# Edge lines kept as sum and difference in a fused spectral mixer: narrower filter products and strided evictions

## The chip, the cores and the metric

The kernel runs on one core of a Trainium2 chip. The metric is the device time of one execution in microseconds (us); lower is better. The engines are named as in the profile: PE is TensorE (PEld its weight loads), DVE is VectorE, ACT is ScalarE, SP is the queue that issues nearly all transfers. L967 is line 967 of the kernel before.

## The reference, cut to what matters

Two branches are mixed by a gate that is computed per row. Branch A is a two-dimensional real FFT, a product with a complex filter, and the inverse FFT. Branch B is a layer norm and a two-layer network over the token axis.

```python
x = A_x                                       # [1, 2048, 512], bf16
g = sigmoid((x * gate_w).sum(-1, keepdims=True))
X = rfft2(x)                                  # over tokens S = 2048 and features D = 512
X = X * (w_r + 1j * w_i)                      # filter [2048, 257]
a = irfft2(X, s=(S, D))
h = layernorm(B_x)
u = gelu(einsum("bsd,sf->bdf", h, w1) + b1)   # F = 1792
b = transpose(einsum("bdf,fs->bds", u, w2) + b2)
out = g * a + (1 - g) * b
```

## The kernel before, in words

The 2048 tokens are split as q (4) x position (128 partitions) x r (4), so there are 16 row blocks of 128 rows, numbered j = 4q + r. Every step of the kernel is added as a task with an engine, a duration that the author has set, what it reads and writes, the PSUM banks it takes (`fa`, `fb`, `acc`) and a priority. A list scheduler (`Plan.order`) then writes out the order of all engines from these. So an edit of a duration can move instructions on every engine. `mm(...)` is the duration of a group of matmuls.

The network is two runs of 512-column matmuls: `m1` (L705, 16 row blocks for each of 14 tiles of hidden units) and `m2` (L1008, 14 tiles for each of 16 row blocks). They are independent of the FFT branch until the final sum and stand between its steps on PE.

The FFT branch runs as follows.

- Forward transforms (`fa`, `fb`) as matmuls with tables of cosines and sines, with butterflies on DVE between them. The columns 0 and 256 of the spectrum, the two edge lines, are packed together into column 0 of the buffer `B`.
- The filter: `wfn` (L767) mirrors column 256 of the filter with four matmuls of 2 columns, and L770 evicts them. `wprep` (L777 to L781) halves one row of the filter and adds up its ends. `nyq` (L801 to L804) multiplies the one line at the Nyquist row. `c0a`, `c0b`, `c0c` (L846) take the edge lines out, multiply them, and write them back to column 0 of `B`.
- A small product for the edge rows (`linem`, L858), whose result goes back into `B` by a transfer on SP.
- First inverse, over tokens: `i1` (L890 for odd r; L895, L897, L898 for even r) from `B` with the table `ti`, evicted by `i1ev` (L904, L906), then butterflies `zf` (L914 to L920) and `fq` (L926, L927) on DVE.
- Last inverse, over features: `i3` (L967 to L970) from `xp` with the table `tg`. For each row block it makes 512 values in one bank: a half with even rows (256 columns, of which 129 get a second matmul on top) and a half with odd rows (two times 128 columns). `i3ev` (L974) on ACT scales them by the gate into the buffer `B`, and `es` (L989 to L993) on DVE forms the sums and differences that are the 512 features.
- `yev` (L1014) on ACT evicts the network's rows with the other gate, L1027 adds the two branches, and for the last two row blocks L1021 on DVE does both. Stores follow.

The i3 groups go by pairs of row blocks, one in bank `fa`, one in `fb`; each tag has two buffers, so a pair waits until the pair two before it has been evicted.

In the half with even rows, position 0 and position 128 of the 129 cosine columns and the 127 sine columns stand in order d = 0, 1, 2, ...

Of the kernel before, what the change touches and what calls it, by code (L numbers as in the profile page):

```python
# [34 lines left out]
def make_tables():  # L35

    p = np.arange(P)
    r4 = np.arange(4)
    alt = np.where(p % 2 == 0, 1.0, -1.0)

    def ang(rows, k, n):
        return 2 * np.pi * ((rows[..., None] * k) % n) / n

    ta = np.zeros((P, 4, 640))
    ti = np.zeros((P, 3072))
    for r in range(4):
# [12 lines left out]
        o, w = ti_at(r)  # L59
        v = ti[:, o:o + w]  # L60
        if r % 2:
            sg = np.where(p < 64, 1.0, -1.0)[:, None]
            th = ang(k, s, S)
            v = v.reshape(P, 7, P)
            v[:, 0] = np.cos(th)
            v[:, 1] = sg * np.cos(th)
            v[:, 2] = -np.sin(th)
            v[:, 3] = -sg * np.sin(th)
            v[0, 2:4] = alt * (0.5 ** 0.5 if r == 1 else -(0.5 ** 0.5))
            th = ang(1 + 4 * (p ^ 96), s, S)  # L70
            v[:, 4] = -np.sin(th)
            v[:, 5] = np.cos(th)
            v[:, 6] = np.sin(th)
            ti[:, o:o + w] = v.reshape(P, w)
        else:
            s5 = np.append(s, 512)
            for lt, kk in enumerate((k, 1 + 4 * (p ^ 96))):
                th = ang(kk, s5, S)
                c, n = np.cos(th), -np.sin(th)
                if lt == 0:  # L80
                    n[0, 0:P] = 0.0 if r == 0 else -alt
                u = v[:, 256 * lt:256 * lt + 256]
                u[:, 0:P], u[:, P:] = c[:, 0:P], n[:, 0:P]
                if r == 0:
                    u[:, P] = c[:, P] if lt == 0 else -n[:, P]
    ti[:, 2945:3072] = ti[:, 129:256]
    ti[0, 2816:2945] = np.append(alt, 1.0)

    tb = np.zeros((P, 2, 2, 3, 64))
    for par in range(2):  # L90
        for h in range(2):
            th = ang(2 * p + h, par + 2 * np.arange(64), D)
            tb[:, par, h, 0] = np.cos(th)
            tb[:, par, h, 1] = -np.sin(th)
            if par == 0:
                tb[:, 0, h, 1, 0] = (alt, -alt)[h]
            tb[:, par, h, 2] = tb[:, par, h, 0]
    cf = np.zeros((P, 4, 2))
    m = np.arange(8).reshape(4, 2)
    for r in range(4):  # L100
        cf[m[0, 0], r, 0] = 1.0
        cf[8, r, 0] = (1.0, -1.0)[r % 2]
        cf[m[1, r % 2], r, 0] = (1.0, -1.0, -1.0, 1.0)[r]
        if r != 2:
            cf[m[2, 0], r, 1], cf[m[3, 0], r, 1] = 1.0, (1.0, -1.0)[r % 2]
        if r != 0:
            cf[m[2, 1], r, 1], cf[m[3, 1], r, 1] = (0.0, -1.0, 1.0, 1.0)[r], (0.0, -1.0, -1.0, 1.0)[r]
    tb = np.concatenate([tb.reshape(P, 768), cf.reshape(P, 8)], 1)

    tg = np.zeros((P, 642))  # L110
    sc = 2.0 / (D * S)
    d = np.arange(129)
    for h in range(2):
        th = ang(2 * p + h, d, D)
        c, n = sc * np.cos(th), -sc * np.sin(th)
        if h == 0:
            c[0], n[0] = sc / 2, 0.0
            tg[:, 513:642], tg[:, 129:256] = c, n[:, 1:128]
        else:
            tg[:, 256:384], tg[:, 384], tg[:, 385:512] = c[:, 0:128], -n[:, 128], n[:, 1:128]  # L120
    tg[0, 0:129] = np.where(d % 2 == 0, 1.0, -1.0) * sc / 2
    return {"flip": bf(np.eye(P)[::-1]), "ta": bf(ta), "ti": bf(ti), "tb": bf(tb), "tg": bf(tg)}


# [122 lines left out]
def d1(n):  # L247
    return 0.07 + n / 960.0
# [4 lines left out]


def mm(*ns):
    return sum(max(n, 120) / 2400.0 + 0.0025 for n in ns)

# [7 lines left out]
def kernel(  # L265
# [192 lines left out]
    def ld_ti():  # L458
        t["ti"] = sb([P, 3072], BF16, "rot")
        dma(t["ti"][:], tabs["ti"])  # L460
    load("tg", [P, 642], BF16, tabs["tg"], 164352, prio=39.5)


    def xe(r):
# [297 lines left out]
                add("ACT", act(512), wfe, reads=[("pw", comp, lt, a)], writes=[("W~", comp, lt)], prio=3, free=[tag])  # L762

    def wfn():
        pw = t["pwn"] = ps([P, 4, 2], F32, "fa", 2)
        for e in range(4):
            T.matmul(pw[:, e], lhsT=t["flip"][:], rhs=t["wt"][:, :, 3 - e, 256], start=True, stop=True)  # L767
    add("PE", mm(*[4] * 4), wfn, reads=[("wt", 0), ("wt", 1), "flip"], writes=["pwn"], prio=5, alloc=["fa"])
    wtk = [("W~", comp, 0) for comp in range(2)]
    add("ACT", 0.3, lambda: A.copy(t["W"][:, :, 0, :, 1, 256], t["pwn"][:].rearrange("p e k -> p k e")),  # L770
        reads=["pwn"], writes=wtk, prio=3, free=["fa"])

    pbk = [("pb", lt, e, c) for lt in range(2) for e in range(4) for c in range(2)]

    def wprep():
        W, pm = t["W"], t["wpm"]
        V.tensor_scalar_mul(W[0:1, :, 0, 0, :, 0:257], W[0:1, :, 0, 0, :, 0:257], 0.5)  # L777
        ends = [W[:, comp].rearrange("p a e s l -> p (a e) s l")[:, :, :, 0:257:256] for comp in range(2)]
        pv = [pm[:, i].rearrange("p a e k -> p (a e) k") for i in range(2)]
        V.tensor_add(pv[0], ends[0][:, :, 0], ends[0][:, :, 1])  # L780
        V.tensor_sub(pv[1], ends[1][:, :, 0], ends[1][:, :, 1])  # L781
    add("DVE", 0.8, wprep, reads=[], writes=[("W", 0), ("W", 1), "wpm"] + wtk, prio=1)


    for lt in range(2):
# [8 lines left out]
        if lt == 0:  # L794
            def nyq():
# [5 lines left out]
                    V.tensor_mul(na[:, i], v, wn[:, i, None, 0:L].to_broadcast([1, 2, L]))  # L801
                V.tensor_sub(nn[:, 0], na[:, 0, 1], na[:, 1, 0])
                V.tensor_add(nn[:, 1], na[:, 1, 1], na[:, 0, 0])
                V.tensor_mul(nn[:, :, 0], t["c0"][0:1, 0, 0, 1, :], wn[:, 0, 0:257:256])  # L804
            add("DVE", 3 * d1(512) + 0.1, nyq, reads=[("B", i, e) for i in range(2) for e in range(4)] + [("W", 0), ("W", 1), ("c0", 0)] + pbk, writes=["nn"], prio=0.5)

        def c0b(lt=lt):
            c0, cm, ce, pm = t["c0"][:, lt], t["cm"], t["ce"][:, lt], t["wpm"]
# [34 lines left out]
        add("DVE", tt(2048) + 2 * tt(1024), ob, reads=["xs"], writes=bk, prio=pr)  # L843

        def c0c(lt=lt):
            V.tensor_copy(t["B"][:, lt, :, :, 0], t["ce"][:, lt].rearrange("p e c k -> p e (c k)"))  # L846
        add("DVE", 0.15, c0c, reads=[("ce", lt)], writes=bk, prio=pr)

        if lt == 0:
            def lines():  # L850
# [22 lines left out]
    for rs, h in ((0, 0), (0, 1), (1, 0), (1, 1)):  # L873
        for r in (rs, rs + 2):
            for lt in range(2):
                tag = ("fa", "fb")[lt]

                def i1(h=h, r=r, lt=lt, tag=tag):
# [6 lines left out]
                    for v in range(2):  # L885
# [3 lines left out]
                                f = (2 * c if lt == 0 else 5 - c) * P  # L889
                                T.matmul(p1[:, v], lhsT=d(c), rhs=ti[:, f:f + L], start=(c == 0), stop=(c == 1))  # L890
                        else:
                            n = 129 if r == 0 and lt == 0 else P
                            u = ti[:, 256 * lt:256 * lt + 256]
                            if n > P:
                                T.matmul(p1[:, v], lhsT=d(1), rhs=t["ti"][:, 2816:3072], start=True, stop=False)  # L895
                            else:
                                T.matmul(p1[:, v, n:], lhsT=d(1), rhs=u[:, n:], start=True, stop=True)  # L897
                            T.matmul(p1[:, v, 0:n], lhsT=d(0), rhs=u[:, 0:n], start=(n == P), stop=True)  # L898
                i1t[h, r, lt] = add("PE", mm(*([256] * 4 if r % 2 else [128] * 4)), i1, reads=[("T", lt, r % 2), "ti"] + ([("T", lt, 1)] if r == 2 else []), writes=[("i1", h, r, lt)], prio=3, alloc=[tag])

                def i1ev(h=h, r=r, lt=lt):
                    if r % 2:
                        o = t["zz"][:, 1, h, lt, :, :, r // 2, :]
                        A.copy(o, t["i1", h, r, lt][:].rearrange("p v (k a) -> p v k a", k=2))  # L904
                    else:
                        A.copy(t["ze"][:, h, r // 2, lt], t["i1", h, r, lt][:])  # L906
                add("ACT", act(512), i1ev, reads=[("i1", h, r, lt)] + pbk, writes=[("zz" if r % 2 else "ze", h, r, lt)], prio=1.7, free=[tag], after=[lined])

            if r % 2 == 0:
# [47 lines left out]
    for p in range(NJ // 2):  # L957
# [4 lines left out]
        def i3(j0=j0, j1=j1, rs=rs):  # L962
            g = t["tg"]
            for n, j in enumerate((j0, j1)):
                p3 = t["i3", j] = ps([P, 2, L], F32, ("fa", "fb")[n], 2)
                zv = [xph(h)[:, 2048 * rs:2048 * rs + 2048].rearrange("p (q v r a) -> p q v r a", q=4, v=2, r=2)[:, j // 4, :, n, :] for h in range(2)]
                T.matmul(p3[:, 0], lhsT=zv[0][:, 1], rhs=g[:, 0:256], start=True, stop=False)  # L967
                T.matmul(p3[:, 0, 0:129], lhsT=zv[0][:, 0], rhs=g[:, 513:642], start=False, stop=True)
                T.matmul(p3[:, 1, 0:128], lhsT=zv[1][:, 0], rhs=g[:, 256:384], start=True, stop=True)
                T.matmul(p3[:, 1, 128:256], lhsT=zv[1][:, 1], rhs=g[:, 384:512], start=True, stop=True)  # L970
        add("PE", mm(*[128] * 6, 256, 256), i3, reads=[("z", rs, 0), ("z", rs, 1), "tg"], writes=[("i3", j0), ("i3", j1)], prio=4, alloc=["fa", "fb"])
        for n, j in enumerate((j0, j1)):
            def i3ev(j=j, n=n, p=p):
                A.activation(eo_v(p)[:, n], t["i3", j][:], ActF.Copy, scale=t["g"][:, j:j + 1])  # L974
            add("ACT", act(512, 1), i3ev, reads=[("i3", j), "g"] + ([("eo", j0)] if n else []), writes=[("eo", j)], prio=1.5, free=[("fa", "fb")[n]],
                after=[i1t[h, r, lt] for h in range(2) for r in (rs, rs + 2) for lt in range(2)])

# [98 lines left out]
```

## Time and profile before

| | before |
|---|---|
| time of three runs, us | 127.7, 127.93, 128.27 (median 127.93) |
| profiled execution, us | 128.01, of which 126.2 is the span from the first to the last instruction |
| granted PE clock | 0.999 |
| PE busy | 121.4 us, 743 matmuls |
| DVE busy | 114.4 us, 273 instructions |
| ACT busy | 81.0 us, 165 instructions |
| last inverse on PE (first i3 to the last) | 99.95 to 109.80 us |

Times in a timeline row are the start, then the duration. Matmuls overlap in the pipeline, so a matmul's price in a stream is the step from its start to the next start and not its duration. The same holds for ACT and DVE, where an instruction's record runs on for about 0.1 us into the next one.

### The profile page before, as it was taken

To read this page: it belongs to the slowest core of one execution; us is meant where nothing else is said; L and a number is where in the kernel's file an instruction comes from. 1 tells how busy PE (TensorE), PEld (TensorE's weight loads), DVE (VectorE), ACT (ScalarE), POOL (GpSimd) and SP (SyncE) were. 2 spreads that over 40 slices of the span, in tenths; PEclk is the share of its full clock that TensorE was granted. 3 is DMA by queue.
4 is the path that set the end of the run, shared out by engine and by line. 5 is a ranking of instruction groups with operands and counts; after the bars stand their busy time and mean duration, and the time that the engine had idled before them with its cause. 6 is when DMAs were issued, how large, how long until landed. Compare 5 with 4: busy or idle time off the path is not lost.

```text
span 126.2 us, 2141 instructions
## 1 busy us (share of the span) xinstructions
PE 121.4 (96%) x743; PEld 68.9 (55%) x756; DVE 114.4 (91%) x273; ACT 81.0 (64%) x165; POOL 0.2 (0%) x4
## 2 busy tenths in 40 slices
PE   6999999999999999999999999999999999999991
PEld 2244555555655466654455555555577767655590
DVE  2599999999999999999999999999988999999951
ACT  0972689699999999999520004732299999952200
POOL 0000000000000000000000000000000000000000
PEclk9999999999999999999999999999999999999999
DMA  2999999996367964599999940000000000021751
GB/s 63 266 368 363 379 363 362 349 330 89 99 124 225 275 133 112 125 393 412 413 408 409 407 173 0 0 5 0 3 0 0 0 5 0 0 82 58 280 208 44
DMA packets 18220, 23.12 MB, mean 183 GB/s; under 512 B 2191, under 2 KB 15905, under 8 KB 18209
## 3 DMA queue, kind: packets, MB, share of 16 engines
q1 hardware_dynamic: 17616, 22.36, 53.3%
q10 hardware_dynamic: 592, 0.62, 2.0%
q8 instruction: 6, 0.10, 0.3%
q14 instruction: 6, 0.04, 0.1%
HBM read 20.86 MB, written 2.10 MB: 182 GB/s over the span
## 4 chain that ended last, share of the span: by engine, by line
PE 93%; DMA 3%; ACTq 1%; issue 1%; DVE 0%
PE acc L1008 32%; PE acc L705 30%; PE fb L705 5%; PE fb L1008 5%; PE fa L705 3%; DMA wa<-in_B_w_dram 3%; PE fa L554 2%; PE fb L653 2%; PE fa L653 2%; PE fa L890 2%; PE fb L890 1%; PE fa L555 1%; ACTq L306 1%; PE fa L557 1%; PE fa L556 1%
## 5 line engine op out<-in xcount | busy, mean ns | idle before, releaser
L705 PE MATMUL acc<-h,wb 128*128 128x512 bf16 x108 | 25.9, 379 | 0.1
L1008 PE MATMUL acc<-gl,wb 128*128 128x512 bf16 (+1 forms) x94 | 24.0, 371 | 0.2
L1008 PE MATMUL acc<-gl,wa 128*128 128x512 bf16 (+1 forms) x97 | 23.8, 371 | 0.1
L1014 ACT ACTIVATE x<-acc,ombb,omg 128x512 bf16<-128x512 f32 x12 | 9.1, 782 | 21.2 <-PE acc L1008 21.2
L1008 PEld LDWEIGHTS <-wa 128*128 128x128 bf16 x126 | 13.5, 113 | 9.9
L1008 PEld LDWEIGHTS <-wb 128*128 128x128 bf16 x126 | 13.3, 113 | 9.3
L705 PE MATMUL acc<-h,wa 128*128 128x512 bf16 x62 | 17.5, 382 | 0.1
L705 PEld LDWEIGHTS <-wb 128*128 128x128 bf16 x112 | 10.7, 98 | 10.5
L705 PEld LDWEIGHTS <-wa 128*128 128x128 bf16 x112 | 10.3, 98 | 10.7 <-DMA wa<-in_B_w_dram 1.0
L487 DVE BATCH_NORM_STATS2 stats<-x 128x6 f32<-128x512 bf16 x14 | 9.5, 678 | 2.5 <-DMA x<-in_A_x_dram 2.5
L560 ACT CAST xp<-fa 128x512 bf16<-128x512 f32 x16 | 9.1, 582 | 2.0 <-PE fa L557 2.0
L735 ACT ACTIVATE x<-x 128x512 bf16<-128x512 bf16 x16 | 10.2, 691 | 0.0
L721 ACT ACTIVATE gl<-acc,b1f 128x512 bf16<-128x512 f32 x11 | 7.9, 718 | 3.2 <-PE acc L705 3.2
L705 PE MATMUL fb<-h,wa 128*128 128x512 bf16 x31 | 9.5, 379 | 0.1
L527 ACT ACTIVATE h<-x,nmr,rstd 128x512 bf16<-128x512 bf16 x11 | 8.4, 807 | 1.1 <-DMA wb<-in_B_w_dram 0.8
L705 PE MATMUL fa<-h,wa 128*128 128x512 bf16 x16 | 6.1, 393 | 0.1
L653 PEld LDWEIGHTS <-X 128*128 128x128 bf16 x64 | 4.7, 98 | 2.1
L974 ACT ACTIVATE B<-fb,g 128x512 bf16<-128x512 f32 x8 | 5.7, 713 | 0.0
L974 ACT ACTIVATE B<-fa,g 128x512 bf16<-128x512 f32 x8 | 5.6, 706 | 0.1
L356 PE MATMUL fa<-xp 128*128 128x512 bf16 x10 | 4.4, 631 | 1.2 <-DVE xp L317 1.2
L660 ACT CAST X<-fb 128x512 bf16<-128x512 f32 x8 | 5.1, 636 | 0.0
L511 ACT ACTIVATE rstd<-mv,eps 128x1 f32<-128x1 f32 (+1 forms) x11 | 3.2, 293 | 2.9 <-DVE mv L488 2.4
(169 smaller groups left out, 234.6 us busy)
## 6 DMA issues: line engine op xcount, KB each, us to landing
wb<-in_B_w_dram SPq DMA_DIRECT2D x11, 512.0 KB
wa<-in_B_w_dram SPq DMA_DIRECT2D x7, 512.0 KB
wa<-in_B_w_dram SPq DMA_DIRECT2D x2, 896.0 KB
wb<-in_B_w_dram SPq DMA_DIRECT2D x4, 384.0 KB
out_dram<-x SPq DMA_DIRECT2D x3, 512.0 KB
x<-in_A_x_dram SPq DMA_DIRECT2D x2, 512.0 KB
wa<-in_B_w_dram SPq DMA_DIRECT2D x2, 448.0 KB
rot<-dft_ti SPq DMA_DIRECT2D x1, 768.0 KB
```

What stands on the lines that cost most here:

```text
L356: T.matmul(pw[:], lhsT=t["warm"][:, 0:P], rhs=t["warm"], start=True, stop=True)
L487: V.bn_stats(out=t["stats"][:, j, :], in_=t["x"][:, j // 4, j % 4, :])
L527: add("ACT", 0.71, lambda j=j: A.activation(t["h"][:, j // 4, j % 4, :], t["x"][:, j // 4, j % 4, :], ActF.Identity, bias=t["nmr"][:, j:j ...
L560: add("ACT", act(512), lambda r=r, dq=dq: A.copy(xe(r)[:, :, :, dq, :], t["pa", r, dq][:]), reads=[("pa", r, dq)], writes=[("X", r, dq)], ...
L653: T.matmul(pb[:, k % 2, k // 2], lhsT=t["X"][:, lt, EX[e], c, k, :], rhs=tbl(k, c), start=True, stop=True)
L660: A.copy(t["X"][:, lt, EX[e]].rearrange("p c j l -> p (c j l)").rearrange("p (h c g b) -> p h c g b", h=2, c=2, b=2)[:, :, c], t["pb", lt, ...
L705: T.matmul(t["u", ft][:], lhsT=w[:, j // 4, j % 4, c * P:(c + 1) * P], rhs=t["h"][:, j // 4, j % 4, :], start=(j == jorder[0]), stop=(j == ...
L721: gelus.append(add("ACT", act(512, 1) , lambda ft=ft: A.activation(t["gl"][:, ft, :], t["u", ft][:], ActF.Gelu_apprx_tanh, bias=t["b1f"][: ...
L735: A.activation(t["x"][:, q, r, :], t["x"][:, q, r, :], ActF.Copy, accum_out=t["glog"][:, 4 * q + r:4 * q + r + 1])
L974: A.activation(eo_v(p)[:, n], t["i3", j][:], ActF.Copy, scale=t["g"][:, j:j + 1])
L1008: T.matmul(t["y", j, m][:, cs], lhsT=w[:, o, 512 * q + r:512 * q + 512:4], rhs=t["gl"][:, ft, cs], start=(ft == 0), stop=(ft == NFT - 1))
L1014: A.activation(tbuf(j).rearrange("p h d -> p (h d)"), t["y", j, 0][:], ActF.Identity, bias=t["ombb2"][:, j:j + 1], scale=t["omg"][:, j:j + 1])
```

## The change

Column 0 of `B` now holds the sum and the difference of the two edge lines instead of the lines themselves. `c0c` forms them (two small operations in place of a copy), the Nyquist line gets two one-element operations, and the halving of a filter row (L777) moves into the tables. In both inverses the even and the odd output positions of the half with the edge lines then need different sources, so they are kept apart: the output of a group is ordered by parity, even positions first, and in place of 256 + 129 columns there are 191 + 64 + 65 (`i3` for all 16 row blocks; `i1` for r = 0, lt = 0). The evictions `i3ev` and that one `i1ev` read PSUM in order and write every second element, which restores the order for DVE. The two 128-column matmuls of the other half write two runs of 64. The four products of `wfn` become one of 8 columns. The planner's least cost of a matmul goes from 120 columns to 62, and the durations of the edited tasks are adapted. The tables `ti`, `tb` and `tg` change with it.

```diff
 def mm(*ns):
-    return sum(max(n, 120) / 2400.0 + 0.0025 for n in ns)
+    return sum(max(n, 62) / 2400.0 + 0.0025 for n in ns)
...
+    cf[:, 0] = cf[:, 0] @ np.array([[1.0, 1.0], [1.0, -1.0]])
+    cf[0:2] *= 0.5
...
     def wfn():
-        pw = t["pwn"] = ps([P, 4, 2], F32, "fa", 2)
-        for e in range(4):
-            T.matmul(pw[:, e], lhsT=t["flip"][:], rhs=t["wt"][:, :, 3 - e, 256], start=True, stop=True)
+        pw = t["pwn"] = ps([P, 2, 4], F32, "fa", 2)
+        T.matmul(pw[:], lhsT=t["flip"][:], rhs=t["wt"][:, :, :, 256], start=True, stop=True)
...
-    add("ACT", 0.3, lambda: A.copy(t["W"][:, :, 0, :, 1, 256], t["pwn"][:].rearrange("p e k -> p k e")),
+    add("ACT", 0.3, lambda: A.copy(t["W"][:, :, 0, :, 1, 256], t["pwn"][:, :, ::-1]),
...
     def wprep():
-        V.tensor_scalar_mul(W[0:1, :, 0, 0, :, 0:257], W[0:1, :, 0, 0, :, 0:257], 0.5)
...
-                V.tensor_mul(nn[:, :, 0], t["c0"][0:1, 0, 0, 1, :], wn[:, 0, 0:257:256])
+                V.tensor_mul(pz[:, 0:2], t["c0"][0:1, 0, 0, 1, :], wn[:, 0, 0:257:256])
+                V.tensor_add(nn[:, 0, 0:1], pz[:, 0:1], pz[:, 1:2])
+                V.tensor_sub(nn[:, 1, 0:1], pz[:, 0:1], pz[:, 1:2])
...
         def c0c(lt=lt):
-            V.tensor_copy(t["B"][:, lt, :, :, 0], t["ce"][:, lt].rearrange("p e c k -> p e (c k)"))
+            b, ce = t["B"][:, lt], t["ce"][:, lt]
+            V.tensor_add(b[:, :, 0:4:2, 0], ce[:, :, :, 0], ce[:, :, :, 1])
+            V.tensor_sub(b[:, :, 1:4:2, 0], ce[:, :, :, 0], ce[:, :, :, 1])
...
-                            n = 129 if r == 0 and lt == 0 else P
                             u = ti[:, 256 * lt:256 * lt + 256]
-                            if n > P:
-                                T.matmul(p1[:, v], lhsT=d(1), rhs=t["ti"][:, 2816:3072], start=True, stop=False)
+                            if r == 0 and lt == 0:
+                                T.matmul(p1[:, v, 65:256], lhsT=d(1), rhs=t["ti"][:, 2816:3007], start=True, stop=False)
+                                T.matmul(p1[:, v, 128:192], lhsT=d(0), rhs=u[:, 66:130], start=False, stop=True)
+                                T.matmul(p1[:, v, 0:65], lhsT=d(0), rhs=u[:, 0:65], start=True, stop=True)
...
-                        A.copy(t["ze"][:, h, r // 2, lt], t["i1", h, r, lt][:])
+                        o, i = t["ze"][:, h, r // 2, lt], t["i1", h, r, lt][:]
+                        if r == 0 and lt == 0:
+                            o, i = o.rearrange("p v (n w) -> p v w n", w=2), i.rearrange("p v (w n) -> p v w n", w=2)
+                        A.copy(o, i)
...
-                T.matmul(p3[:, 0], lhsT=zv[0][:, 1], rhs=g[:, 0:256], start=True, stop=False)
-                T.matmul(p3[:, 0, 0:129], lhsT=zv[0][:, 0], rhs=g[:, 513:642], start=False, stop=True)
-                T.matmul(p3[:, 1, 0:128], lhsT=zv[1][:, 0], rhs=g[:, 256:384], start=True, stop=True)
-                T.matmul(p3[:, 1, 128:256], lhsT=zv[1][:, 1], rhs=g[:, 384:512], start=True, stop=True)
-        add("PE", mm(*[128] * 6, 256, 256), i3, ...)
+                ph = p3[:, 1].rearrange("p (w n) -> p w n", w=2)
+                gh = g[:, 322:578].rearrange("p (c w n) -> p c w n", c=2, w=2)
+                T.matmul(p3[:, 0, 65:256], lhsT=zv[0][:, 1], rhs=g[:, 0:191], start=True, stop=False)
+                T.matmul(p3[:, 0, 128:192], lhsT=zv[0][:, 0], rhs=g[:, 258:322], start=False, stop=True)
+                T.matmul(p3[:, 0, 0:65], lhsT=zv[0][:, 0], rhs=g[:, 192:257], start=True, stop=True)
+                for c in range(2):
+                    T.matmul(ph[:, :, 64 * c:64 * c + 64], lhsT=zv[1][:, c], rhs=gh[:, c], start=True, stop=True)
+        add("PE", mm(*[191, 64, 65, 128, 128] * 2), i3, ...)
...
-                A.activation(eo_v(p)[:, n], t["i3", j][:], ActF.Copy, scale=t["g"][:, j:j + 1])
+                A.activation(eo_v(p)[:, n].rearrange("p h (n w) -> p h w n", w=2), t["i3", j][:].rearrange("p h (w n) -> p h w n", w=2), ActF.Copy, scale=t["g"][:, j:j + 1])
```

More of the change, by code (lines that the diff above doesn't have):

```diff
@@ L83, in make_tables @@
                 u[:, 0:P], u[:, P:] = c[:, 0:P], n[:, 0:P]
[L84 to L87, printed above, removed]
+                if r == 0 and lt:
+                    u[:, P] = -n[:, P]
+                elif r == 0:
+                    ti[:, 2816:2879], ti[:, 2943:3007] = n[:, 2:P:2], n[:, 1:P:2]
+                    u[:, 0:65], u[:, 66:130] = c[:, 0:129:2], c[:, 1:P:2]
+                    u[0, 66:130], ti[0, 2879:2943] = 0.0, 1.0
     tb = np.zeros((P, 2, 2, 3, 64))
@@ L107, in make_tables @@
             cf[m[2, 1], r, 1], cf[m[3, 1], r, 1] = (0.0, -1.0, 1.0, 1.0)[r], (0.0, -1.0, -1.0, 1.0)[r]
+    cf[:, 0] = cf[:, 0] @ np.array([[1.0, 1.0], [1.0, -1.0]])
+    cf[0:2] *= 0.5
     tb = np.concatenate([tb.reshape(P, 768), cf.reshape(P, 8)], 1)
-    tg = np.zeros((P, 642))
+    tg = np.zeros((P, 578))
     sc = 2.0 / (D * S)
@@ L116, in make_tables @@
         if h == 0:
-            c[0], n[0] = sc / 2, 0.0
-            tg[:, 513:642], tg[:, 129:256] = c, n[:, 1:128]
-        else:
-            tg[:, 256:384], tg[:, 384], tg[:, 385:512] = c[:, 0:128], -n[:, 128], n[:, 1:128]
-    tg[0, 0:129] = np.where(d % 2 == 0, 1.0, -1.0) * sc / 2
+            tg[:, 0:63], tg[:, 127:191] = n[:, 2:128:2], n[:, 1:128:2]
+            tg[:, 192:257], tg[:, 258:322] = c[:, 0:129:2], c[:, 1:128:2]
+            tg[0] = 0.0
+            tg[0, 63:127] = tg[0, 192:257] = sc / 2
+        else:
+            tg[:, 322:386], tg[:, 386:450] = c[:, 0:128:2], c[:, 1:128:2]
+            tg[:, 450], tg[:, 451:514], tg[:, 514:578] = -n[:, 128], n[:, 2:128:2], n[:, 1:128:2]
     return {"flip": bf(np.eye(P)[::-1]), "ta": bf(ta), "ti": bf(ti), "tb": bf(tb), "tg": bf(tg)}
@@ L460, in ld_ti @@
         dma(t["ti"][:], tabs["ti"])
-    load("tg", [P, 642], BF16, tabs["tg"], 164352, prio=39.5)
+    load("tg", [P, 578], BF16, tabs["tg"], 147968, prio=39.5)
     def xe(r):
@@ L764, in wfn @@
     def wfn():
-        pw = t["pwn"] = ps([P, 4, 2], F32, "fa", 2)
-        for e in range(4):
-            T.matmul(pw[:, e], lhsT=t["flip"][:], rhs=t["wt"][:, :, 3 - e, 256], start=True, stop=True)
-    add("PE", mm(*[4] * 4), wfn, reads=[("wt", 0), ("wt", 1), "flip"], writes=["pwn"], prio=5, alloc=["fa"])
+        pw = t["pwn"] = ps([P, 2, 4], F32, "fa", 2)
+        T.matmul(pw[:], lhsT=t["flip"][:], rhs=t["wt"][:, :, :, 256], start=True, stop=True)
+    add("PE", mm(8), wfn, reads=[("wt", 0), ("wt", 1), "flip"], writes=["pwn"], prio=5, alloc=["fa"])
     wtk = [("W~", comp, 0) for comp in range(2)]
-    add("ACT", 0.3, lambda: A.copy(t["W"][:, :, 0, :, 1, 256], t["pwn"][:].rearrange("p e k -> p k e")),
+    add("ACT", 0.3, lambda: A.copy(t["W"][:, :, 0, :, 1, 256], t["pwn"][:, :, ::-1]),
         reads=["pwn"], writes=wtk, prio=3, free=["fa"])
@@ L781, in wprep @@
         V.tensor_sub(pv[1], ends[1][:, :, 0], ends[1][:, :, 1])
-    add("DVE", 0.8, wprep, reads=[], writes=[("W", 0), ("W", 1), "wpm"] + wtk, prio=1)
+    add("DVE", 0.4, wprep, reads=[], writes=[("W", 0), ("W", 1), "wpm"] + wtk, prio=1)
     for lt in range(2):
@@ L803, in nyq @@
                 V.tensor_add(nn[:, 1], na[:, 1, 1], na[:, 0, 0])
-                V.tensor_mul(nn[:, :, 0], t["c0"][0:1, 0, 0, 1, :], wn[:, 0, 0:257:256])
-            add("DVE", 3 * d1(512) + 0.1, nyq, reads=[("B", i, e) for i in range(2) for e in range(4)] + [("W", 0), ("W", 1), ("c0", 0)] + pbk, writes=["nn"], prio=0.5)
+                V.tensor_mul(pz[:, 0:2], t["c0"][0:1, 0, 0, 1, :], wn[:, 0, 0:257:256])
+                V.tensor_add(nn[:, 0, 0:1], pz[:, 0:1], pz[:, 1:2])
+                V.tensor_sub(nn[:, 1, 0:1], pz[:, 0:1], pz[:, 1:2])
+            add("DVE", 3 * d1(512) + 0.35, nyq, reads=[("B", i, e) for i in range(2) for e in range(4)] + [("W", 0), ("W", 1), ("c0", 0)] + pbk, writes=["nn"], prio=0.5)
         def c0b(lt=lt):
@@ L845, in c0c @@
         def c0c(lt=lt):
-            V.tensor_copy(t["B"][:, lt, :, :, 0], t["ce"][:, lt].rearrange("p e c k -> p e (c k)"))
-        add("DVE", 0.15, c0c, reads=[("ce", lt)], writes=bk, prio=pr)
+            b, ce = t["B"][:, lt], t["ce"][:, lt]
+            V.tensor_add(b[:, :, 0:4:2, 0], ce[:, :, :, 0], ce[:, :, :, 1])
+            V.tensor_sub(b[:, :, 1:4:2, 0], ce[:, :, :, 0], ce[:, :, :, 1])
+        add("DVE", 0.3, c0c, reads=[("ce", lt)], writes=bk, prio=pr)
         if lt == 0:
@@ L891, in i1 @@
                         else:
-                            n = 129 if r == 0 and lt == 0 else P
                             u = ti[:, 256 * lt:256 * lt + 256]
-                            if n > P:
-                                T.matmul(p1[:, v], lhsT=d(1), rhs=t["ti"][:, 2816:3072], start=True, stop=False)
-                            else:
-                                T.matmul(p1[:, v, n:], lhsT=d(1), rhs=u[:, n:], start=True, stop=True)
-                            T.matmul(p1[:, v, 0:n], lhsT=d(0), rhs=u[:, 0:n], start=(n == P), stop=True)
-                i1t[h, r, lt] = add("PE", mm(*([256] * 4 if r % 2 else [128] * 4)), i1, reads=[("T", lt, r % 2), "ti"] + ([("T", lt, 1)] if r == 2 else []), writes=[("i1", h, r, lt)], prio=3, alloc=[tag])
+                            if r == 0 and lt == 0:
+                                T.matmul(p1[:, v, 65:256], lhsT=d(1), rhs=t["ti"][:, 2816:3007], start=True, stop=False)
+                                T.matmul(p1[:, v, 128:192], lhsT=d(0), rhs=u[:, 66:130], start=False, stop=True)
+                                T.matmul(p1[:, v, 0:65], lhsT=d(0), rhs=u[:, 0:65], start=True, stop=True)
+                            else:
+                                T.matmul(p1[:, v, P:], lhsT=d(1), rhs=u[:, P:], start=True, stop=True)
+                                T.matmul(p1[:, v, 0:P], lhsT=d(0), rhs=u[:, 0:P], start=True, stop=True)
+                i1t[h, r, lt] = add("PE", mm(*([256] * 4 if r % 2 else [128] * 4 if r or lt else [191, 64, 65] * 2)), i1, reads=[("T", lt, r % 2), "ti"] + ([("T", lt, 1)] if r == 2 else []), writes=[("i1", h, r, lt)], prio=3, alloc=[tag])
                 def i1ev(h=h, r=r, lt=lt):
@@ L966, in i3 @@
                 zv = [xph(h)[:, 2048 * rs:2048 * rs + 2048].rearrange("p (q v r a) -> p q v r a", q=4, v=2, r=2)[:, j // 4, :, n, :] for h in range(2)]
[L967 to L971, printed above, removed]
+                ph = p3[:, 1].rearrange("p (w n) -> p w n", w=2)
[5 more added lines that the diff above has]
+                    T.matmul(ph[:, :, 64 * c:64 * c + 64], lhsT=zv[1][:, c], rhs=gh[:, c], start=True, stop=True)
+        add("PE", mm(*[191, 64, 65, 128, 128] * 2), i3, reads=[("z", rs, 0), ("z", rs, 1), "tg"], writes=[("i3", j0), ("i3", j1)], prio=4, alloc=["fa", "fb"])
         for n, j in enumerate((j0, j1)):
             def i3ev(j=j, n=n, p=p):
-                A.activation(eo_v(p)[:, n], t["i3", j][:], ActF.Copy, scale=t["g"][:, j:j + 1])
+                A.activation(eo_v(p)[:, n].rearrange("p h (n w) -> p h w n", w=2), t["i3", j][:].rearrange("p h (w n) -> p h w n", w=2), ActF.Copy, scale=t["g"][:, j:j + 1])
             add("ACT", act(512, 1), i3ev, reads=[("i3", j), "g"] + ([("eo", j0)] if n else []), writes=[("eo", j)], prio=1.5, free=[("fa", "fb")[n]],
```

## The prediction, made before the changed kernel had run

> **What bounds the kernel now.** I read the page first (busy time, chain), then TensorE's waits, then the timeline of each engine where the change sits.
>
> ```profile
> span 126.2 us, 2141 instructions
> ...
> PE 121.4 (96%) x743; PEld 68.9 (55%) x756; DVE 114.4 (91%) x273; ACT 81.0 (64%) x165; POOL 0.2 (0%) x4
> ...
> PE 93%; DMA 3%; ACTq 1%; issue 1%; DVE 0%
> ```
>
> TensorE (PE) carries 93% of the chain that ended last. VectorE (DVE), at 91%, carries none of it, so it is busy beside PE and not ahead of it. The only wait that the list of waits gives for PE's matmuls is this one, at the start:
>
> ```profile
> PE fa L356 <- DVE xp L317: 1.2, 1, 1.2
> ```
>
> I also followed PE's starts from 36 to 123 us. Each matmul starts where the one before it lets it, except at ten places with a hole of 0.21 us, which is one 512-column matmul whose record is missing. So from 36 us on a nanosecond taken from PE's stream is a nanosecond of the end, as long as no operand comes late. The question is what the new stream costs, and what comes late.
>
> The stream's prices are its steps from start to start. Half a pair of the last inverse (four matmuls into one bank, then the first of the next bank):
>
> ```profile
> 100.51 0.27 PE L967 MATMUL fa<-tg,xp 128*128 128x256 bf16 x1
> 100.62 0.22 PE L968 MATMUL fa<-tg,xp 128*128 128x129 bf16 x1
> 100.68 0.22 PE L969 MATMUL fa<-tg,xp 128*128 128x128 bf16 x1
> 100.73 0.22 PE L970 MATMUL fa<-tg,xp 128*128 128x128 bf16 x1
> 100.79 0.27 PE L967 MATMUL fb<-tg,xp 128*128 128x256 bf16 x1
> ```
>
> The steps, taken finer from all sixteen such groups, are 0.109 us for 256 columns, 0.057 for 129, 0.057 and 0.056 for 128: 0.279 us a row block. The small filter product is the shortest matmul in the trace:
>
> ```profile
> 53.99 0.24 PE L767 MATMUL fa<-wt,flip 128*128 128x2 bf16 x4
> 54.10 0.38 PE L705 MATMUL acc<-h,wb 128*128 128x512 bf16 x1
> ```
>
> Four matmuls of 2 columns, each with its own weight load, take 54.10 - 53.99 = 0.11 us (finer, 0.107): steps of 0.029 and three of 0.026. That is PE's smallest step here.
>
> **The change, part by part.** *Last inverse, 16 row blocks.* 256 + 129 columns become 191 + 64 + 65, and the two 128s stay (written in two runs of 64; L556 writes so already and steps at 0.056). From 129 to 256 columns the step grows by (0.109 - 0.057)/127 = 0.41 ns a column, so 191 columns cost 0.0825 us. For 64 and 65 columns the trace has no row. The bounds are 0.026 (2 columns) and 0.056 (128). Going down from 128 at 0.41 ns a column gives 0.030, close to the lower bound, which shows that a weight load does not hold the step above 0.026; I take 0.029 and 0.030. A block is then 0.0825 + 0.029 + 0.030 + 0.113 = 0.2545, which is 0.0245 less; times 16, **-0.39 us**. With 0.026 for both it is 0.0315 less a block, with 0.056 it is 0.0285 more.
>
> The Trainium skill ("TensorE: Matmul & The Clock Gate", Back-to-back issue gap) speaks against such a split: in a stream of weight loads and matmuls it gives about 81 ns for 128 columns, as the load counts too. This trace differs: 0.056 us at 128 columns with a load before each. With 0.081 for every matmul of 128 columns or fewer a block would cost 0.0545 more than before.
>
> *First inverse.* Four groups (r = 0, lt = 0; two h, two v) get the same new shapes for 256 + 129:
>
> ```profile
> 91.00 0.27 PE L895 MATMUL fa<-rot,B 128*128 128x256 bf16 x1
> 91.11 0.22 PE L898 MATMUL fa<-rot,B 128*128 128x129 bf16 x1
> 91.17 0.27 PE L895 MATMUL fa<-rot,B 128*128 128x256 bf16 x1
> ```
>
> Again 0.0245 each: **-0.10 us** (-0.13 to +0.11).
>
> *Filter product.* Four matmuls become one of 8 columns: 0.107 to 0.029, **-0.08 us**. Its eviction (L770) keeps its 8 elements.
>
> *Vector work.* L777 goes (57.77 to 58.22 on DVE, 0.45 us). Two one-element operations come in for the Nyquist line and one more 8-element operation in each of the two edge-line writes; such operations step at 0.07 to 0.12 us (L809 to L814), so 0.3 to 0.5 comes back. I count nothing. What hides it is PE's feed-forward work ahead of the first inverse. DVE's L591 ended at 92.05 and PE used it at 92.54, and the edge-line transfer had landed at 90.24 for a weight load at 90.79, a margin of half a microsecond at both; without that cover the cost would be the balance itself, from 0.15 us gained to 0.05 lost. The table transfers keep their places (one is 16 KB smaller), and no queue is passed.
>
> *Order.* The built program keeps 66 feed-forward matmuls between the edge-line product and the first inverse, and 16 inside the inverse; one of its groups comes three such matmuls later and the butterflies run as r = 0, r = 2 for each h. PE would reach the last inverse 0.08 + 0.10 = 0.18 us sooner. Its first pair started at 99.95, when DVE's L927 had ended at 99.82: a margin of 0.13. DVE starts on L914 when ScalarE (ACT) delivers, ACT on PE's first groups, so this chain moves forward with PE (about 0.17), and the new order leaves DVE no more idle time than its 0.41 us before L919. I count no wait here.
>
> *Stores at a stride.* The 16 evictions L974 and two of L906 write every second bf16. No ACT row of 512 elements writes so. At the lower end they cost what they cost (0.57 us a step). At the upper end each element takes twice its time: L770, 8 elements, lets the next start after 0.06 us, and 512 elements step at 0.475 (L904), so elements are some 0.42 us of a step. Below nothing there is nothing to be had, since PE doesn't wait for ACT. The nearest row with this stride in SBUF is a read, the weight loads of L890 (every second column of B), beside those of packed data:
>
> ```profile
> L890 PEld LDWEIGHTS <-B 128*128 128x128 bf16 x32 | 3.1, 98 | 0.9
> L970 PEld LDWEIGHTS <-xp 128*128 128x128 bf16 x16 | 1.6, 98 | 0.0
> ```
>
> Both take 98 ns. I take nothing for the stride. The Trainium skill ("SBUF — State Buffer", Door 1: The DMA port swizzle) says that bf16 can be strided by up to 8 elements free of charge; no run here shows it for a store.
>
> Where a dearer store would strike:
>
> ```profile
> 108.41 0.69 ACT L974 ACTIVATE B<-fb,g 128x512 bf16<-128x512 f32 x1
> ...
> 109.53 0.27 PE L967 MATMUL fb<-tg,xp 128*128 128x256 bf16 x1
> ```
>
> The second bank of the last pair waits for the twelfth eviction, done at 109.10: margin 0.43. In the new order I lay both chains out from the first pair's start. PE: seven pairs of 0.509 and 26 feed-forward matmuls of 0.2157 bring the last pair to 9.17 us, its second bank to 9.43. ACT: first eviction at 0.45, eleven steps of 0.57, two of 0.66 for feed-forward results between them, so the twelfth starts at 8.04 and is done at 8.75. Margin 0.68, some 0.6 after a semaphore.
>
> *The end.* DVE must keep up with a PE that ends sooner:
>
> ```profile
> 119.50 0.68 DVE L1027 TENSOR_TENSOR x<-x,B 128x1024 bf16<-128x1024 bf16 x1
> 120.36 0.75 DVE L1021 SCALAR_TENSOR_TENSOR x<-acc,omg,x 128x512 bf16<-128x512 f32 x1 [0.18 <-PE acc L1008]
> 121.89 0.48 DVE L1021 SCALAR_TENSOR_TENSOR x<-acc,omg,x 128x256 bf16<-128x256 f32 x1 [0.78 <-PE acc L1008]
> ```
>
> It idles 0.18 and 0.78 us before the first two final sums. With PE 0.57 sooner the first may be DVE-bound, but the second keeps 0.96 - 0.57 = 0.39 of margin.
>
> **Sum.** -0.39 - 0.10 - 0.08 = **-0.57 us**. The profiled execution took 128.01 us (span 126.2, 1.8 around it) and would take 127.44; it stands 0.08 above the median of 127.93, which would become **127.4**.
>
> **Rivals.** *A (forecast)*: PE's columns, no new wait; with both short steps between 0.026 and 0.030 it is -0.57 to -0.71, that is 127.2 to 127.4. For it: no stall from 36 us on, and the 0.026 row. Chance 0.71.
>
> *B: short matmuls are held up by their weight loads.* Every step of 64 or 65 columns is 0.056: 20 groups times 0.0285 = +0.57, less 0.08, +0.49: 128.4. For it: 64 columns with alternating weights appear nowhere, and L767 loads the same matrix four times. Against: those loads are still issued, at 97 ns each, and start 0.026 apart. Chance 0.06. The 81 ns of the Trainium skill's TensorE page would make it 20 x 0.0545 - 0.24 = +0.85, an estimate of 128.8.
>
> *C: strided stores are slower, and ACT paces the last inverse.* With x more for each eviction the last pair comes 12x - 0.6 late: nothing up to x = 0.05, no gain left at x = 0.10, 0.5% slower at x = 0.15. At x = 0.42 it is 12 x 0.42 - 0.6 - 0.57 = +3.9, near 131.8. For it: ACT runs without a pause there, and the store pattern is new. Against: the equal weight loads. Chance 0.18.
>
> *D: the new order makes the first pair of the last inverse wait.* If DVE did not come sooner, 0.18 - 0.13 = 0.05 is lost; if it comes later by one pair of butterflies (L919 and L920, 0.68 us), 0.73: 127.4 to 128.1. Against: the idle 0.41 that the new order can use. Chance 0.05.
>
> **How the numbers follow.** The forecast is A, 127.4. The range runs from A's lower end less the spread of the runs (127.2 - 0.2) to B: 127.0 to 128.4; it holds A, B and D, 0.82, and leaves C out. About 0.5%, 0.64 us, is what a measurement of this kernel can tell from no change. A lies at that line: its sum is 0.07 short of it, its other end 0.07 beyond, and the runs scatter by more, so I split it 0.40 faster to 0.31 within. B and D fall within, 0.11, and so does C with a small x, 0.02; C with a large x is the slower 0.16. Together 0.40, 0.44, 0.16.
>
> **What would show it.** In the profile after: steps of 0.08, 0.03, 0.03 for 191, 64 and 65 columns; one L767 row in place of four; L974's successor at a step of 0.57; no wait of PE from 36 us on; the first pair of the last inverse about 0.18 us sooner and the last matmul about 0.57. The forecast is wrong if short steps read 0.05 (B), if evictions step above 0.62 and PE waits for them (C), or if PE waits for DVE near 99.8 (D).

## The result, and the profile after

The kernel became a little slower: 128.24 us (median of 22 runs) against 127.84 for the kernel before (median of 22 runs). The ratio is 1.0040, with a 95% interval of 1.0029 to 1.0051, which is 0.37 to 0.65 us; the quotient of the two medians alone is 1.0031. The forecast was 127.4. The profiled execution took 128.14 us, of which 126.4 is the span. Line numbers below are those of the changed kernel, 15 higher at the end of the file: `i3` is L981 to L985, its eviction L989, the network's matmuls L711 and L1023, the network's eviction L1029.

The page first, with the same three lines as before:

```profile
span 126.4 us, 2191 instructions
...
PE 122.1 (97%) x773; PEld 68.8 (54%) x773; DVE 114.2 (90%) x276; ACT 83.2 (66%) x165; POOL 0.2 (0%) x4
...
PE 84%; ACT 10%; ACTq 2%; issue 1%; DVE 1%
```

ScalarE, which was on none of the chain but for its queue, now carries 10% of it. Where, the chain in order of time shows, from 90 us on (its longest pieces: start, duration, what):

```profile
100.37 1.23 ACT B L989 x2
103.09 4.28 ACT B L989 x6
107.99 2.10 ACT B L989 x3
110.55 11.46 PE acc L1023 x60
```

The ACT pieces are the strided evictions of the last inverse. For these 7.6 us the end hung on ACT and not on PE, which does not mean that the kernel lost 7.6 us: what it lost is the time that PE stood waiting. ACT's and PE's rows around the last pair show how:

```profile
108.48 0.92 ACT L989 ACTIVATE B<-fa,g 128x512 bf16<-128x512 f32 x1
109.16 0.92 ACT L989 ACTIVATE B<-fb,g 128x512 bf16<-128x512 f32 x1
...
109.81 0.27 PE L985 MATMUL fa<-tg,xp 128*128 128x128 bf16 x2
...
110.13 0.24 PE L981 MATMUL fb<-tg,xp 128*128 128x191 bf16 x1
```

An eviction now steps to the next in 0.67 to 0.71 us, where it was 0.57. The twelfth one (started at 109.16) is done at 110.08, and PE begins the second bank of the last pair at 110.13; it could have begun 0.21 earlier. The same happens at four pairs: PE's step between the banks is 0.11, 0.21, 0.23 and 0.21 us too long, 0.76 in all. The list of waits names none of this for PE; only the chain and the steps do.

The first inverse has two strided evictions of its own (L918 for r = 0, lt = 0; L906 in the kernel before), and PE waits twice for a bank. ACT's row in the kernel before, and the rows of the changed kernel:

```profile
91.53 1.79 ACT L906 CAST h<-fa 128x512 bf16<-128x512 f32 x3 [1.49 <-PE fa L898]
```

```profile
91.31 2.02 ACT L918 CAST h<-fa 128x512 bf16<-128x512 f32 x3 [1.66 <-PE fa L904]
91.33 0.81 PE L1023 MATMUL acc<-gl,wb 128*128 128x512 bf16 x3
...
92.10 0.24 PE L902 MATMUL fa<-rot,B 128*128 128x191 bf16 x1
```

Three matmuls of 512 columns last 0.65, so L902 could have started at 91.98; it waited 0.12, and a later one (L898) 0.11. The three copies, of which the first and the third are strided, take 2.02 us here and took 1.79 before; a strided one steps at 0.60 where a packed one steps at 0.48.

PE's own stream did nearly what was worked out. A group of the last inverse, and the filter product, which is now one row:

```profile
100.17 0.24 PE L981 MATMUL fb<-tg,xp 128*128 128x191 bf16 x1
100.26 0.19 PE L982 MATMUL fb<-tg,xp 128*128 128x64 bf16 x1
100.28 0.19 PE L983 MATMUL fb<-tg,xp 128*128 128x65 bf16 x1
100.31 0.28 PE L985 MATMUL fb<-tg,xp 128*128 128x128 bf16 x2
100.43 0.24 PE L981 MATMUL fa<-tg,xp 128*128 128x191 bf16 x1
```

```profile
53.67 0.18 PE L772 MATMUL fa<-wt,flip 128*128 128x8 bf16 x1
53.70 0.81 PE L711 MATMUL acc<-h,wb 128*128 128x512 bf16 x3
```

The steps are 0.082 for 191 columns, 0.028 for 64, 0.029 for 65 (0.035 in 7 of 16 groups), 0.055 to 0.061 for 128, and 0.029 for the 8 columns of the filter product. Where PE doesn't wait, a block takes 0.257 us on average (0.255 to 0.260), against 0.278 in the kernel before. So PE's columns gained 0.34 us in the last inverse, 0.09 in the first and 0.08 in the filter product, 0.51 in all.

The sum of what the profile shows is -0.51 (PE's columns) + 0.76 + 0.23 (waits) = +0.48 us. The medians differ by 0.40, and the sum lies within the interval of 0.37 to 0.65.

### The profile page after: what moved, and what is told of

It reads as the page before. It is cut to its first block, busy times and chain, and to the rows that moved or that the text cites. A ratio compares the mean times of both kernels' runs of the same rounds, so it can differ in the third digit from the quotient of the medians.

```text
span 126.4 us, 2191 instructions
## 1 busy us (share of the span) xinstructions
PE 122.1 (97%) x773; PEld 68.8 (54%) x773; DVE 114.2 (90%) x276; ACT 83.2 (66%) x165; POOL 0.2 (0%) x4
## 4 chain that ended last, share of the span: by engine, by line
PE 84%; ACT 10%; ACTq 2%; issue 1%; DVE 1%
PE acc L711 29%; PE acc L1023 28%; ACT B L989 6%; PE fb L1023 5%; PE fb L711 5%; PE fa L711 3%; ACTq L312 2%; PE fa L560 2%; PE fa L898 1%; PE fa L659 1%; PE fb L659 1%; PE fb L898 1%; PE fa L561 1%; ACT x L1029 1%; ACT L367 1%
## 5 line engine op out<-in xcount | busy, mean ns | idle before, releaser
L711 PE MATMUL acc<-h,wb 128*128 128x512 bf16 x112 | 26.8, 379 | 0.0
L1023 PE MATMUL acc<-gl,wb 128*128 128x512 bf16 (+1 forms) x98 | 24.3, 371 | 0.0
L1023 PE MATMUL acc<-gl,wa 128*128 128x512 bf16 (+1 forms) x98 | 23.5, 371 | 0.0
L1029 ACT ACTIVATE x<-acc,ombb,omg 128x512 bf16<-128x512 f32 x12 | 9.2, 794 | 19.8 <-PE acc L1023 19.8
L1023 PEld LDWEIGHTS <-wa 128*128 128x128 bf16 x126 | 13.4, 113 | 10.2
L1023 PEld LDWEIGHTS <-wb 128*128 128x128 bf16 x126 | 13.2, 113 | 9.3
L711 PE MATMUL acc<-h,wa 128*128 128x512 bf16 x64 | 17.6, 379 | 0.0
L711 PEld LDWEIGHTS <-wb 128*128 128x128 bf16 x112 | 10.7, 98 | 10.6
L711 PEld LDWEIGHTS <-wa 128*128 128x128 bf16 x112 | 10.3, 98 | 10.4 <-DMA wa<-in_B_w_dram 1.0
L711 PE MATMUL fb<-h,wa 128*128 128x512 bf16 x32 | 9.7, 379 | 0.0
L989 ACT ACTIVATE B<-fa,g 128x512 bf16<-128x512 f32 x8 | 7.2, 897 | 0.1
L989 ACT ACTIVATE B<-fb,g 128x512 bf16<-128x512 f32 x8 | 7.2, 902 | 0.0
L711 PE MATMUL fa<-h,wa 128*128 128x512 bf16 x16 | 6.0, 383 | 0.0
L666 ACT CAST X<-fa 128x512 bf16<-128x512 f32 x8 | 5.0, 622 | 0.0
```

Source lines behind the costliest of these rows:

```text
L666: A.copy(t["X"][:, lt, EX[e]].rearrange("p c j l -> p (c j l)").rearrange("p (h c g b) -> p h c g b", h=2, c=2, b=2)[:, :, c], t["pb", lt, ...
L711: T.matmul(t["u", ft][:], lhsT=w[:, j // 4, j % 4, c * P:(c + 1) * P], rhs=t["h"][:, j // 4, j % 4, :], start=(j == jorder[0]), stop=(j == ...
L989: A.activation(eo_v(p)[:, n].rearrange("p h (n w) -> p h w n", w=2), t["i3", j][:].rearrange("p h (w n) -> p h w n", w=2), ActF.Copy, scal ...
L1023: T.matmul(t["y", j, m][:, cs], lhsT=w[:, o, 512 * q + r:512 * q + 512:4], rhs=t["gl"][:, ft, cs], start=(ft == 0), stop=(ft == NFT - 1))
L1029: A.activation(tbuf(j).rearrange("p h d -> p (h d)"), t["y", j, 0][:], ActF.Identity, bias=t["ombb2"][:, j:j + 1], scale=t["omg"][:, j:j + 1])
```

## The experiments

Theory S: storing every second bf16 makes an eviction longer, and ACT paces PE. Its rivals: R, the cause lies in the read, in the four-piece pattern or in the way PE fills the bank; O, the new order of instructions makes PE wait; B, PE's short matmuls are dearer than they look. In the code below `...` stands for what is left out.

**Reorder on the reading side.** The loop order of the two evictions is exchanged, so that ACT reads PSUM alternately from the even and the odd run and stores packed.

```diff
-  A.activation(eo_v(p)[:, n].rearrange("p h (n w) -> p h w n", w=2), t["i3", j][:].rearrange("p h (w n) -> p h w n", w=2), ...)
+  A.activation(eo_v(p)[:, n].rearrange("p h (n w) -> p h n w", w=2), t["i3", j][:].rearrange("p h (w n) -> p h n w", w=2), ...)
...
-  o, i = o.rearrange("p v (n w) -> p v w n", w=2), i.rearrange("p v (w n) -> p v w n", w=2)
+  o, i = o.rearrange("p v (n w) -> p v n w", w=2), i.rearrange("p v (w n) -> p v n w", w=2)
```

> The changed kernel, with the same reordering done on the other side of the eviction: it reads PSUM alternating between the even and the odd run (the pattern of L660 of the kernel before) and writes SBUF packed. Theory S (storing every second bf16 makes an eviction 0.105 us longer, ACT then paces the last inverse, and PE waits 0.76 us there and 0.22 us in the first inverse): eviction step back to 0.57, no wait of PE from 36 us on, 127.84 - 0.57 = 127.3. Theory R (it is the four-piece access that costs, on whichever side, or the new way in which PE fills the bank): the step stays near 0.675 and the time near 128.2. Theory B (PE's new stream itself is dearer than the old one): steps of 64 and 65 columns near 0.05, 128 or more whatever ACT does.

Measured: 127.51 us (median of 12 runs) against 128.05 for the kernel before (median of 35 runs taken alongside, which serve the next three experiments too), ratio 0.9951 (0.9929 to 0.9974). Evictions step at 0.569:

```profile
106.82 0.75 ACT L989 ACTIVATE B<-fb,g 128x512 bf16<-128x512 f32 x1
107.39 0.76 ACT L989 ACTIVATE B<-fa,g 128x512 bf16<-128x512 f32 x1
107.95 0.77 ACT L989 ACTIVATE B<-fb,g 128x512 bf16<-128x512 f32 x1
...
109.29 0.24 PE L981 MATMUL fb<-tg,xp 128*128 128x191 bf16 x1
```

The twelfth eviction (107.95) is done 0.57 us ahead of the second bank of the last pair, and PE's starts show no wait from 36 us on. S holds. R, taken as a four-piece pattern that costs on either side, falls, since the same pieces cost nothing on the reading side; taken as the way PE fills the bank it falls too, since the filling is the changed kernel's. B falls, since the same PE stream is faster. The -0.54 of the medians agrees with the -0.51 that PE's steps gave and with the forecast's -0.57. The time itself is 0.2 above the expected 127.3, as the kernel before stood 0.2 higher here too (128.05 against 127.84). This version is faster than the kernel before by 0.5%.

**The store alone, in the kernel before.** Only the eviction of the last inverse is changed.

```diff
-  A.activation(eo_v(p)[:, n], t["i3", j][:], ActF.Copy, ...)
+  A.activation(eo_v(p)[:, n].rearrange("p h (n w) -> p h w n", w=2), t["i3", j][:].rearrange("p h (w n) -> p h w n", w=2), ActF.Copy, ...)
```

> The kernel before, with the 16 evictions of the last inverse written at a stride of two (PE's stream, tables and order as before; the 512 values of a row block therefore land in another order than they should, so part of the reordering is changed). Theory S: step 0.57 to 0.675; the last pair's twelfth eviction comes 12 x 0.105 = 1.26 us later, of which ACT's idle 0.17 and the margin of 0.43 take 0.60, so PE waits some 0.66 us in the last inverse and the time is 127.84 + 0.66 = 128.5. Theory R with the bank's filling as cause: step 0.57, 127.84. Theory O (the new order of instructions makes PE wait, and not the price of the store): 127.84.

Measured: 128.77 us, ratio 1.0047 (1.0027 to 1.0067), or +0.60 us. Evictions step at 0.67 to 0.71, and PE waits at four pairs for 0.15, 0.16, 0.16 and 0.19 us, 0.66 in all. The last pair:

```profile
108.92 0.94 ACT L974 ACTIVATE B<-fb,g 128x512 bf16<-128x512 f32 x1
...
109.91 0.27 PE L967 MATMUL fb<-tg,xp 128*128 128x256 bf16 x1
```

The eviction ends at 109.86, PE goes on at 109.91. So the store is enough by itself, without the new stream, tables or order. O falls as the cause, and so does the filling of the bank.

**The changed kernel without reordering.** Both evictions read and write packed.

```diff
+  A.activation(eo_v(p)[:, n], t["i3", j][:], ActF.Copy, ...)
...
-  o, i = o.rearrange("p v (n w) -> p v w n", w=2), i.rearrange("p v (w n) -> p v w n", w=2)
```

> The changed kernel with evictions that read and write packed, so the reordering by parity is left out and the values stay sorted by parity. Theory S: as the run that reads at a stride, step 0.57 and 127.3; the difference between the two is the price of the alternating read. Theory R with the four-piece access as cause: step 0.57, 127.3, while the run that reads at a stride stays at 0.675; with the bank's filling as cause: 0.675 and 128.2. Theory O: 128.2, since the order is the changed kernel's.

Measured: 127.65 us, ratio 0.9965 (0.9944 to 0.9986); evictions step at 0.569 to 0.570, and PE's starts show no wait from 36 us on:

```profile
106.68 0.74 ACT L989 ACTIVATE B<-fb,g 128x512 bf16<-128x512 f32 x1
107.25 0.75 ACT L989 ACTIVATE B<-fa,g 128x512 bf16<-128x512 f32 x1
107.82 0.76 ACT L989 ACTIVATE B<-fb,g 128x512 bf16<-128x512 f32 x1
```

The alternating read of the first experiment steps the same, so from PSUM it is free to the nanosecond that the trace gives; the two ratios' intervals overlap.

**The same store, planned at its price.** The kernel computes the same as the changed one; only the planner is told that the strided evictions last longer.

```diff
-  add("ACT", act(512, 1), i3ev, ...)
+  add("ACT", act(512, 1) + 0.105, i3ev, ...)
...
-  add("ACT", act(512), i1ev, ...)
+  add("ACT", act(512) + 0.105 * (r == 0 and lt == 0), i1ev, ...)
```

> The changed kernel, computing the same, with the planner told 0.105 us more for each of the 18 strided evictions, so that it may put more of the network's matmuls between the pairs of the last inverse. Theory S: evictions still step at 0.675, but PE's waits of 0.76 us in the last inverse and 0.22 in the first shrink to 0.2 or less in all, 127.3 to 127.5; ACT's last eviction comes later, at some 113 us, which DVE needs only near 116. Theory R agrees with S here. Theory B: no change against 128.2, as PE is busy anyhow.

Measured: 127.68 us, ratio 0.9969 (0.9947 to 0.9992). Evictions still step at 0.67 to 0.70, yet PE's starts show no wait from 36 us on. Between the pairs there is now more of the network's work where ACT needs the time (the third pair started 2.10 us after the first in the changed kernel; here it is 2.33):

```profile
100.36 0.25 PE L981 MATMUL fa<-tg,xp 128*128 128x191 bf16 x1
...
101.83 1.03 PE L1023 MATMUL acc<-gl,wa 128*128 128x512 bf16 x4
102.69 0.25 PE L981 MATMUL fa<-tg,xp 128*128 128x191 bf16 x1
```

So the store costs ACT time that ACT has to spare. The kernel lost by it because the order was laid out for evictions of 0.57.

**How far the price goes.** The kernel before with four patterns of store, in turn by pairs: stride 4, stride 8, runs of two and runs of four with gaps as long.

```diff
-  A.activation(eo_v(p)[:, n], t["i3", j][:], ActF.Copy, ...)
+  f, i = eo_v(p)[:, n].rearrange(...), t["i3", j][:].rearrange(...)
+  if p % 4 < 2:
+      w = (4, 8)[p % 4]
+      o, i = f.rearrange("p (n w) -> p w n", w=w), i.rearrange("p (w n) -> p w n", w=w)
+  else:
+      k = (2, 4)[p % 4 - 2]
+      o, i = f.rearrange("p (n w k) -> p w n k", w=2, k=k), i.rearrange("p (w n k) -> p w n k", w=2, k=k)
+  A.activation(o, i, ActF.Copy, ...)
```

> The kernel before, with the 16 evictions of the last inverse stored in four patterns, four evictions each: stride 4, stride 8, runs of two elements with gaps of two, runs of four with gaps of four (the values land in another order than they should, so the order of a row block is changed). The packed step is 0.57, stride 2 measured 0.675. Theory S1 (the price is for every single element that isn't next to the one before): stride 4 and 8 step at 0.675, runs of two at some 0.62, runs of four at 0.60. Theory S2 (the price grows with the bytes that a store reaches over): stride 4 near 0.78, stride 8 near 0.99, runs of two and four at 0.675. Theory S3 (only halves of a 4-byte word are dear): runs of two and of four are back at 0.57, stride 4 and 8 at 0.675.

Measured in one run of 136.94 us (two of the four evictions of each pattern, then the dearest one; L1021 is a network eviction between them):

```profile
100.51 1.43 ACT L981 ACTIVATE B<-fa,g 128x512 bf16<-128x512 f32 x1
101.66 1.41 ACT L981 ACTIVATE B<-fb,g 128x512 bf16<-128x512 f32 x1
102.81 2.57 ACT L981 ACTIVATE B<-fa,g 128x512 bf16<-128x512 f32 x1
104.87 0.93 ACT L1021 ACTIVATE x<-acc,ombb,omg 128x512 bf16<-128x512 f32 x1
105.69 2.52 ACT L981 ACTIVATE B<-fb,g 128x512 bf16<-128x512 f32 x1
107.69 0.94 ACT L981 ACTIVATE B<-fa,g 128x512 bf16<-128x512 f32 x1
108.51 0.69 ACT L981 ACTIVATE B<-fb,g 128x512 bf16<-128x512 f32 x1
109.07 0.71 ACT L981 ACTIVATE B<-fa,g 128x512 bf16<-128x512 f32 x1
109.64 0.71 ACT L981 ACTIVATE B<-fb,g 128x512 bf16<-128x512 f32 x1
...
115.43 2.78 ACT L981 ACTIVATE B<-fb,g 128x512 bf16<-128x512 f32 x1
117.71 0.93 ACT L981 ACTIVATE B<-fa,g 128x512 bf16<-128x512 f32 x1
```

Stride 4 steps at 1.13 to 1.15, stride 8 at 2.0 to 2.3. The instruction after a stride of 8 steps at 0.82; past it, runs of two and of four step at 0.565 to 0.570, as packed ones do. None of the three theories fits whole. S1 falls, as the price grows with the stride. S2 has the direction, but it gave 0.78 and 0.99, and no price was seen for runs. S3 is right for runs and wrong for strides. What is shown: stores of single bf16 elements cost more the farther apart they lie, and runs of two (4 bytes) or of four cost nothing more. Why is open.

**Is it contention with DVE?** Twelve copies of 512 bf16, SBUF to SBUF, are put ahead of ACT's work in the kernel before (the code is shortened, the comments are added here).

```diff
+  for k in range(3): A.copy(f[...], t["warm"])                                   # packed
+  for k in range(3): A.copy(f[...].rearrange("p (n w) -> p w n", w=2), ...)       # stored at stride 2
+  for k in range(3): A.copy(f[...].rearrange("p (n w) -> p w n", w=8), ...)       # stored at stride 8
+  for k in range(3): A.copy(f[...].rearrange("p (n w) -> p n w", w=2), t["warm"].rearrange("p (w n) -> p n w", w=2))
```

> The kernel before with twelve extra copies on ACT at its start, of 512 bf16 each from SBUF to SBUF, when DVE is mostly idle: three packed, three stored at stride 2, three at stride 8, three read in alternation and stored packed. They only lengthen the start (some 6 us). Theory S as a property of ACT's store: stride 2 steps 0.105 us over packed here too. Theory K (the dearer store is a contention with DVE, which is 90% busy in the last inverse and reads the same buffer): stride 2 steps like packed here. The alternating read: like packed in either theory.

Measured in one run (the extra work makes it 141.17 us), ACT's timeline:

```profile
4.59 1.64 ACT L364 COPY gl<-xp 128x512 bf16<-128x512 bf16 x3
6.14 1.99 ACT L366 COPY gl<-xp 128x512 bf16<-128x512 bf16 x3
8.00 6.97 ACT L368 COPY gl<-xp 128x512 bf16<-128x512 bf16 x3
14.47 2.09 ACT L370 COPY gl<-xp 128x512 bf16<-128x512 bf16 x3
```

DVE ended its last instruction at 4.31 and had none until after these. Packed copies step at 0.52, stride 2 at 0.62, stride 8 at 1.95 to 2.26: 0.10 us for stride 2 here too. K falls: the price is there with DVE idle, so it belongs to the store. The alternating read from SBUF steps at 0.573 once the strided stores before it are through (the first takes 0.84), 0.05 over packed.

## Why the prediction was wrong, step by step

- **The step that failed is the store at a stride: "I take nothing for the stride."** It measured x = 0.105 us for each of 16 evictions and 0.12 for the two of the first inverse. PE then waited for ACT to free its banks, 0.76 us in the last inverse and 0.23 in the first, where the forecast A had "no new wait". The bounds that I had (0 and 0.42) held it, but I took the lower end from a row that was not of its kind: a weight load that reads SBUF at the same stride. It says nothing of a store by ACT, as the runs showed: alternating reads are free from PSUM and cost 0.05 from SBUF, stores at stride 2 cost 0.10. The Trainium skill ("SBUF — State Buffer", Door 1: The DMA port swizzle) lets bf16 be strided by up to 8 elements free of charge. The runs don't agree for a store by ACT: 0.10 us more at stride 2 in 0.52, about four times the step at stride 8.
- **Rival C was what happened, with the size near its point of decision.** For x = 0.105 its formula gave a wait of 12 x 0.105 - 0.6 = 0.66 us at the last pair, and 0.76 was measured, spread over four pairs. The margin of "some 0.6" was a little too wide: in the first experiment, with ACT's steps back at 0.57, the twelfth eviction was done 0.57 ahead, of which the hand-over takes 0.05 (done at 110.08, PE at 110.13 in the changed kernel). With 0.52 the formula gives 0.74.
- **A term was left out.** C counted only the last inverse. The two strided evictions of the first one, which I named, also hold banks, and PE waited 0.23 us for them. Neither wait is there in the two experiments that store packed. With 0.66 alone C gave +0.09.
- **PE's columns were nearly right.** A block was to cost 0.2545 and costs 0.257: 64 columns step at 0.028 where 0.029 was taken, but 65 step at 0.035 in 7 of 16 groups, and the 128s at up to 0.061. So the sum of -0.57 should have been -0.51. The first experiment, with nothing but ACT's side mended, gave -0.54 by the medians. B's 0.056 did not come.
- **DVE and the end held.** At the end of the changed kernel DVE idled 0.29 and 0.78 us, but there PE did not end sooner. The test is the first experiment, where it did: DVE had no idle time before the first final sum, as was thought possible, and 0.63 before the second. The first pair of the last inverse came at 99.92, not 0.18 sooner than 99.95. These times also differ from one execution to the next: it was 99.69 in the run of the store alone, whose instructions up to there are the kernel before's. Counted from the edge-line product (L858 at 81.29, L866 at 81.11), the pair came 0.14 later, which is 0.23 of waits less 0.09 of columns. PE did not wait for DVE there (D).
- **What was luck.** The measured 128.24 lies inside the forecast's range, 127.0 to 128.4, but that range was drawn for A, B and D; C was left out of it. The change of 0.4% is also smaller than the 0.5% that the prediction called the least that can be told from no change, an outcome to which it gave 0.44; the interval of 1.0029 to 1.0051 does tell it. None of this speaks for the forecast: the mechanism was C's, which had a chance of 0.18.
- **A count was wrong, without effect.** Between the edge-line product and the first inverse the built programs have 44 of the network's matmuls, not 66. It is the same number in both, which is what the argument used.

## What to carry to other kernels

An engine that is off the chain can still pace it through the buffers it frees: work out the margin of that hand-over, as here 0.57 us over twelve evictions, and ask of every changed access pattern what it adds to one eviction. A reorder that an eviction has to do was best put, in this kernel, on the side that reads PSUM, with a packed store; the kernel before already had such an eviction (L660, 0.475 us a step like the packed L904), and its row was the one to choose by. When an operation does become dearer, tell the planner its measured price before judging the change: with the same store the changed kernel was 0.4% slower than the kernel before when it was planned like a packed one, and 0.3% faster when it was planned 0.105 us dearer.

## What the runs showed of the hardware that was not expected

An eviction by ACT of 512 bf16 from PSUM steps at 0.57 us stored packed, 0.675 at stride 2, 1.13 to 1.15 at stride 4 and 2.0 to 2.3 at stride 8; runs of two or four elements with gaps as long step as packed ones do (0.565 to 0.570). With DVE idle, copies from SBUF to SBUF step at 0.52 packed, 0.62 at stride 2 and 1.95 to 2.26 at stride 8. An alternating read of PSUM between two runs 128 elements apart costs nothing (0.569 against 0.569).
